# Another instruction order and buffer assignment for a transformer block with local dilated attention and SwiGLU on one core

## The chip, the core and the metric

The kernel runs on one core of a Trainium2 chip. The metric is the device time of one execution in microseconds (us), as the median of several runs. The core has five instruction streams that work side by side, each strictly in its own order: TensorE (PE, matrix products into eight PSUM banks), VectorE (DVE), ScalarE (ACT), GpSimd (POOL) and SyncE (SP), which here does nothing but issue DMA transfers. Streams wait for each other through semaphores.

## What is computed

One block with adaptive layer normalisation, for S = 2048 tokens of D = 512 values in bf16:

```python
mod = silu(c) @ w_mod                 # six vectors: sa, ca, ga, sb, cb, gb
h = layernorm(x) * (1 + ca) + sa
x = x + ga * A(h, wqkv, wo)
h = layernorm(x) * (1 + cb) + sb
x = x + gb * B(h, w1, w3, w2)

def A(x, wqkv, wo):                   # H = 32 heads of 16, W = 8 keys, dilation 2
    q, k, v = split_heads(x @ wqkv)
    # token s sees the tokens s, s-2, ..., s-14; those below 0 are masked
    logits = sum_d(q[s] * k[s - 2*w]) * 16 ** -0.5
    o = sum_w(softmax_w(logits) * v[s - 2*w])
    return merge_heads(o) @ wo

def B(x, w1, w3, w2):                 # F = 1792
    return (silu(x @ w1) * (x @ w3)) @ w2
```

## The kernel before

**Tiling.** The tokens lie in 16 tiles of 128. D has four blocks of 128 and F has 14 units of 128. Everything stays on the chip between the stages, but for v, which goes through a scratch buffer in DRAM so that it can be read back at dilated rows.

**Stages.** First 15 warm-up matmuls run, and `first_modulation` makes two of the six vectors from a load of `w_mod`. Then, for the groups of tiles [0,1], [2,3], [4-7], [8-11], [12-15]: `ln_stats` (statistics on DVE at L579 and L580, the reciprocal root on POOL, normalisation on DVE at L600 or ACT), `ln_T` (transposes on PE, or by DMA for the last group, and modulation), `proj_qk` (matmuls at L722, ACT evacuates them at L730 and L733) and `proj_v` (L749, ACT at L759, a store of each v tile to DRAM at L763).

Attention goes by pairs of tiles, the last block having two pairs. `logits` multiplies q by the eight shifted k on DVE into a buffer pq (L780, 128 x 4096 elements, called pq(T) below) and sums over each head on PE (L791, matmuls on parts of the array, called lg(T)). `shift`, `exps` (ACT, L821) and `softmax` (DVE, L833 to L840) follow. `values` loads the shifted v with four DMAs for each tile (L855), multiplies by the softmax on DVE (L862, called av(T)), sums on PE (L871, called acc), evacuates on ACT (L877), transposes by DMA (L878), applies `wo` (L895, four matmuls of 512 columns) and adds to x on DVE (L899).

The FFN goes by the groups [0,1], [2,3], [4-7], [8-11], [12-15]. `ln_sums` normalises again: L610 (DVE), L614 (ACT, once for each tile of a pair), L620 and L621 (POOL), L622 (DVE), L625 (ACT, once for each tile). `ln_T` transposes: from the third group on by DMA (issued by SP, L127 is the helper's line) with the modulation in four ACT instructions at L648. Each of 14 units (`ffn_unit`) has two halves of four matmuls (L911, `w1` and `w3`); ACT applies silu to the one (L917) and copies the other (L921), and DVE multiplies them (L922); in the last group DVE takes the second one straight from PSUM (L925). `ffn_w2` makes the output of each tile with 14 matmuls (L953; L941 for the last two tiles, in pieces), adds x on DVE (L969) and stores (L971).

The remaining vectors come between: `gate(0)` and the scaling of `wo` (L987) by ga, `modulation(1)` (L494 to L502) with its 1 MB load into `wm_s`, `gate(1)` and the scaling of `w2` (L996) by gb.

**Order.** `_build` (L281) records 1151 operations, each with its engine and the values that it reads and writes. `place` (L147) then deals them out: the list `ORDER` (L1018) names all operations in one sequence, and each engine gets its own in that sequence. The list `SLOTS` (L1064) gives each of 590 short-lived values a buffer out of its pool: 8 PSUM banks, 3 buffers for h, 5 for xn, 6 for v, 4 large ones for pq and shifted v (and 2 more that lie over buffers which are free by then), 20 for FFN products and so on. `synchronize` (L169) works out where an engine must wait for another, from true dependencies and from the buffers' earlier users. An operation's place on its engine and its buffer are thus all that the two lists decide:

```python
self.placed = [self.ops[i] for i in order]
for at, o in enumerate(self.placed):
    o.at = at
    o.pos = len(self.order[o.eng])
    self.order[o.eng].append(o)
    for v in o.vals:
        if v.pool is not None and v.pool.last.get(v.slot) is not v:
            before = v.pool.last.get(v.slot)
            if before is not None:
                o.prev.extend(before.users)
            v.pool.last[v.slot] = v
```

Operations are named by their number in the lists: 44 is the load of `wm_s` for the second modulation, 403 to 406 and 413 to 416 are the loads of shifted v for the tiles 0 and 1, 637 and 627 are the output projections of the tiles 15 and 14 (L895), and 798 is the product (L922) of unit 23, the tenth of the FFN's second group.

Of the kernel before, what the change touches and what calls it, by code (L numbers as in the profile page):

```python
# [280 lines left out]
def _build(p, A_x, A_wqkv, A_wo, B_w1, B_w3, B_w2, c, w_mod, out):  # L281
# [737 lines left out]
    15, 20, 1, 5, 7, 8, 16, 6, 17, 4, 2, 21, 58, 3, 22, 23, 28, 24, 25, 31, 32, 10, 11, 12, 13, 14, 0, 63, 64, 65, 66, 67, 87, 88, 89, 59,  # L1019
    60, 90, 68, 69, 70, 71, 92, 93, 91, 94, 61, 72, 62, 101, 19, 95, 161, 73, 163, 78, 74, 75, 79, 76, 96, 164, 162, 165, 80, 97, 102, 98,  # L1020
    77, 99, 103, 105, 115, 116, 120, 121, 106, 100, 166, 104, 107, 108, 168, 26, 81, 122, 123, 167, 169, 173, 27, 170, 82, 84, 83, 171, 174,
    176, 172, 18, 110, 127, 111, 117, 118, 125, 112, 113, 128, 126, 85, 86, 119, 124, 33, 149, 34, 35, 29, 36, 30, 37, 211, 219, 43, 38,
    212, 209, 150, 151, 217, 155, 156, 152, 157, 175, 158, 159, 153, 109, 114, 9, 180, 181, 154, 41, 49, 210, 192, 129, 195, 186, 187, 160,
    44, 198, 130, 201, 182, 218, 40, 144, 405, 220, 265, 188, 145, 45, 267, 42, 266, 139, 202, 203, 146, 147, 213, 183, 184, 140, 185, 196,
    197, 199, 404, 148, 141, 221, 193, 194, 131, 132, 133, 134, 200, 416, 214, 215, 216, 226, 225, 222, 224, 228, 223, 227, 230, 189, 177,
    233, 232, 231, 178, 234, 276, 413, 229, 274, 277, 268, 235, 415, 236, 325, 377, 142, 205, 206, 135, 179, 275, 414, 332, 334, 136, 137,
    333, 403, 190, 191, 406, 249, 251, 143, 378, 247, 253, 138, 323, 278, 269, 270, 271, 279, 273, 324, 272, 289, 280, 281, 285, 282, 207,
    208, 262, 263, 264, 248, 284, 392, 394, 393, 39, 283, 290, 291, 395, 425, 286, 287, 292, 250, 288, 294, 326, 327, 239, 240, 293, 204,
    396, 335, 397, 398, 54, 252, 243, 241, 242, 423, 237, 238, 254, 245, 295, 314, 399, 384, 259, 336, 400, 337, 338, 340, 339, 328, 401,
    297, 343, 329, 330, 341, 331, 402, 385, 417, 260, 261, 303, 299, 379, 315, 301, 380, 305, 300, 342, 52, 407, 302, 244, 246, 381, 344,  # L1030
    426, 418, 424, 304, 408, 419, 454, 420, 317, 296, 409, 427, 428, 256, 382, 386, 309, 306, 410, 320, 456, 318, 429, 430, 257, 421, 310,
    347, 422, 411, 431, 457, 455, 345, 307, 412, 639, 311, 346, 348, 387, 359, 640, 641, 642, 485, 436, 312, 643, 361, 432, 351, 446, 308,
    360, 363, 644, 646, 383, 437, 444, 298, 362, 652, 645, 255, 365, 651, 321, 653, 433, 647, 353, 447, 487, 258, 352, 354, 648, 650, 445,
    649, 371, 448, 372, 654, 368, 369, 449, 488, 450, 435, 434, 438, 486, 439, 440, 458, 459, 50, 47, 51, 316, 460, 357, 358, 355, 489, 490,
    366, 356, 491, 705, 707, 374, 364, 708, 516, 492, 493, 46, 670, 494, 313, 53, 700, 375, 715, 716, 451, 452, 453, 441, 442, 443, 733,
    349, 671, 48, 461, 462, 717, 388, 706, 350, 734, 660, 477, 735, 463, 709, 701, 718, 719, 55, 736, 737, 465, 468, 672, 467, 370, 464,
    665, 661, 666, 685, 687, 688, 466, 478, 475, 673, 690, 695, 686, 696, 738, 476, 702, 703, 655, 389, 697, 674, 740, 739, 704, 710, 711,
    691, 680, 692, 518, 499, 698, 689, 662, 745, 506, 498, 741, 663, 664, 746, 747, 748, 742, 667, 668, 682, 319, 683, 657, 469, 743, 658,
    744, 495, 712, 497, 713, 714, 720, 722, 721, 675, 723, 724, 677, 678, 676, 496, 479, 656, 659, 509, 681, 774, 754, 776, 679, 684, 759,
    761, 777, 762, 508, 470, 471, 519, 517, 480, 520, 756, 507, 481, 760, 764, 669, 725, 729, 755, 765, 757, 482, 521, 522, 763, 578, 472,  # L1040
    758, 500, 538, 775, 778, 528, 693, 769, 789, 779, 780, 781, 56, 782, 791, 792, 799, 801, 800, 802, 699, 790, 766, 767, 510, 483, 484,
    501, 768, 511, 502, 523, 524, 512, 793, 473, 474, 749, 751, 750, 57, 525, 390, 391, 770, 804, 806, 503, 527, 807, 513, 694, 783, 752,
    809, 810, 794, 795, 796, 827, 828, 829, 830, 831, 529, 547, 784, 771, 772, 773, 530, 797, 504, 505, 730, 805, 808, 785, 514, 832, 834,
    540, 833, 539, 322, 367, 803, 537, 811, 515, 786, 787, 526, 844, 835, 836, 837, 838, 726, 839, 812, 753, 798, 814, 843, 815, 816, 817,
    823, 531, 532, 373, 813, 840, 841, 845, 818, 788, 842, 819, 820, 824, 549, 541, 542, 550, 580, 731, 821, 727, 846, 533, 534, 850, 579,
    548, 581, 586, 596, 595, 849, 825, 551, 552, 559, 560, 535, 569, 582, 561, 536, 732, 584, 376, 848, 847, 851, 901, 902, 861, 863, 570,
    862, 881, 864, 882, 883, 884, 885, 852, 856, 857, 853, 865, 854, 568, 553, 606, 543, 906, 866, 891, 558, 855, 571, 607, 587, 544, 554,
    555, 556, 557, 871, 873, 872, 874, 605, 867, 908, 909, 868, 869, 562, 876, 877, 878, 879, 572, 893, 870, 563, 585, 583, 573, 880, 564,
    822, 588, 907, 910, 545, 911, 546, 903, 894, 630, 892, 565, 937, 574, 575, 912, 939, 858, 589, 590, 615, 895, 859, 875, 896, 938, 940,
    904, 886, 888, 566, 887, 889, 860, 728, 629, 576, 941, 942, 929, 943, 616, 577, 617, 944, 898, 567, 945, 619, 597, 632, 618, 631, 947,  # L1050
    897, 913, 620, 946, 948, 949, 591, 592, 593, 916, 917, 918, 919, 925, 914, 915, 950, 933, 954, 899, 953, 905, 952, 921, 956, 920, 951,
    890, 955, 959, 958, 900, 926, 927, 934, 922, 923, 622, 594, 957, 633, 621, 930, 931, 623, 608, 960, 981, 598, 599, 1016, 1018, 1017,
    1019, 1020, 976, 978, 977, 979, 980, 983, 961, 1021, 986, 987, 962, 984, 988, 996, 997, 971, 1006, 989, 982, 1007, 1008, 1009, 963, 609,
    600, 634, 624, 610, 601, 602, 972, 998, 964, 965, 611, 612, 1001, 1011, 1002, 991, 1026, 999, 1000, 603, 604, 932, 935, 635, 636, 992,
    613, 614, 993, 625, 626, 936, 1047, 924, 973, 1049, 990, 974, 1048, 994, 1050, 1027, 1051, 995, 985, 1010, 1052, 1013, 966, 968, 975,
    969, 1054, 637, 1022, 967, 627, 628, 1023, 1024, 928, 1003, 638, 1012, 1055, 1028, 1064, 1056, 1057, 1058, 1059, 970, 1053, 1039, 1035,
    1043, 1031, 1025, 1063, 1014, 1004, 1060, 1062, 1066, 826, 1061, 1029, 1015, 1065, 1070, 1069, 1030, 1005, 1036, 1044, 1037, 1068, 1032,
# [52 lines left out]
```

## Time and profile before

| | us |
|---|---|
| three runs | 239.56, 241.00, 238.92 |
| their median | 239.56 |
| the profiled execution | 239.86 |
| its span, first to last instruction | 237.7 |

The page of the profile gives, for the profiled execution, the busy time of each engine, the same in 40 slices of the span, the queues of the DMA engines, the chain of work that ended last, and the costliest groups of instructions. In such a group stand the line, engine and operation, the output and its inputs, how many instructions it has, their busy time, the mean of one in ns, and the engine's idle time just before them with what ended most of it. The chain shows where the end of the program comes from:

```profile
PE 68%; DVE 12%; DMA 7%; ACT 7%; issue 3%; POOL 1%; SPq 1%; DVEq 0%
```

Followed back from the last instruction, 68% of the span is work of PE. The other view used below is the timeline, which lists runs of equal instructions with their start, their length from the first start to the last end, engine, line and operation, and in brackets how long the engine had been idle before and what released it.

### The profile page before, as it was taken

How to read it: one execution, taken by the hardware profiler on the slowest of the kernel's cores; microseconds unless marked ns; L12 is line 12 of the kernel's file. 1: busy time of each engine (PE TensorE's matmuls, PEld its weight loads, DVE VectorE, ACT ScalarE, POOL GpSimd, SP SyncE). 2: the span in 40 equal slices, each digit the busy share in tenths (PEclk: the TensorE clock that was granted, in tenths of full speed). 3: DMA queues.
4: the chain of work that ended last, by engine and by line, in shares of the span. 5: the costliest groups of instructions: out<-in, count | busy, mean ns of one | idle time of the engine just before them, and what ended most of it. 6: DMA issues, size and time to landing. Idle time of an engine off the chain costs nothing.

```text
span 237.7 us, 4314 instructions
## 1 busy us (share of the span) xinstructions
PE 229.9 (97%) x1665; PEld 120.7 (51%) x1689; DVE 169.8 (71%) x284; ACT 156.4 (66%) x311; POOL 23.1 (10%) x55
## 2 busy tenths in 40 slices
PE   7899998999999999999999999999999999999996
PEld 2667543544568855754434444444344444444454
DVE  4789998999999999999999847379134424042722
ACT  2289798899989987683689799444757926133100
POOL 8323050001001000030000021000001100000000
PEclk9999999999999999999999999999999999999999
DMA  6999999989999977693897484330032142000002
GB/s 185 341 352 351 238 274 179 188 221 297 327 261 273 285 181 223 139 261 69 205 330 116 124 229 105 103 117 0 3 90 88 44 77 80 0 0 0 3 0 88
DMA packets 44731, 38.31 MB, mean 161 GB/s; under 512 B 19736, under 2 KB 36008, under 8 KB 44712
## 3 DMA queue, kind: packets, MB, share of 16 engines
q1 hardware_dynamic: 44656, 38.04, 63.3%
q8 instruction: 13, 0.21, 0.4%
q14 instruction: 6, 0.05, 0.1%
q10 hardware_dynamic: 56, 0.01, 0.0%
HBM read 29.63 MB, written 4.21 MB: 142 GB/s over the span
## 4 chain that ended last, share of the span: by engine, by line
PE 68%; DVE 12%; DMA 7%; ACT 7%; issue 3%; POOL 1%; SPq 1%; DVEq 0%
PE pall L911 38%; PE pall L953 13%; PE pall L722 5%; DMA sb_wo<-in_A_wo_dram 5%; PE pall L895 4%; DVE sb_vsh L862 3%; PE pall L941 3%; DMA sb_wm_s<-in_w_mod_dram 2%; PE pall L871 2%; PE pall L749 2%; ACT sb_h L648 1%; ACT sb_xn L614 1%; PE pall L791 1%; DVE sb_pq L780 1%; DVE sb_pq L862 1%
## 5 line engine op out<-in xcount | busy, mean ns | idle before, releaser
L911 PE MATMUL pall<-sb_h,sb_w 128*128 128x512 bf16 (+1 forms) x554 | 99.6, 336 | 0.5 <-issue 0.2
L911 PEld LDWEIGHTS pall<-sb_h,sb_w 128*128 128x128 bf16 x560 | 52.2, 98 | 47.1 <-ACT sb_sg L917 5.2
L917 ACT ACTIVATE sb_sg<-pall 128x512 bf16<-128x512 f32 (+1 forms) x70 | 33.9, 516 | 29.6 <-PE pall L911 28.6
L953 PE MATMUL pall<-sb_w,sb_hh 128*128 128x512 bf16 x190 | 43.4, 379 | 0.3
L722 PE MATMUL pall<-sb_h,sb_wqkv 128*128 128x512 bf16 (+1 forms) x157 | 30.4, 336 | 1.3 <-ACT sb_v L759 0.8
L953 PEld LDWEIGHTS pall<-sb_w,sb_hh 128*128 128x128 bf16 x196 | 18.9, 98 | 22.7 <-issue 0.4
L921 ACT ACTIVATE sb_hh<-pall 128x256 bf16<-128x256 f32 (+1 forms) x56 | 26.8, 497 | 3.4 <-PE pall L911 3.0
L922 DVE TENSOR_TENSOR sb_hh<-sb_sg,sb_hh 128x256 bf16<-128x256 bf16 (+1 forms) x56 | 17.7, 351 | 12.8 <-ACT sb_hh L921 12.8
L969 DVE TENSOR_TENSOR sb_o<-pall,sb_x 128x512 bf16<-128x512 f32 (+3 forms) x18 | 10.9, 627 | 18.5 <-PE pall L953 13.7
L722 PEld LDWEIGHTS pall<-sb_h,sb_wqkv 128*128 128x128 bf16 x160 | 14.6, 98 | 14.0 <-ACT sb_v L759 1.3
L925 DVE TENSOR_TENSOR sb_hh<-sb_sg,pall 128x512 bf16<-128x512 bf16 x14 | 9.1, 684 | 16.0 <-PE pall L911 15.9
L648 ACT ACTIVATE sb_h<-sb_h,sb_modc 128x512 bf16<-128x512 bf16 x16 | 11.7, 806 | 11.2 <-DMA sb_h<-sb_xn 11.2
L620 POOL TENSOR_SCALAR sb_rs<-sb_var 128x2 f32<-128x2 f32 x8 | 3.4, 427 | 144.4 <-ACT sb_xn L614 144.4
L862 DVE TENSOR_TENSOR sb_pq<-sb_pq,sb_al 128x4096 bf16<-128x4096 bf16 x7 | 15.8, 2285 | 1.0 <-DMA sb_pq<-v_scratch_dram 1.0
L862 DVE TENSOR_TENSOR sb_vsh<-sb_vsh,sb_al 128x4096 bf16<-128x4096 bf16 x7 | 15.9, 2281 | 0.0
L749 PE MATMUL pall<-sb_wqkv,sb_h 128*128 128x512 bf16 x59 | 15.2, 379 | 0.3 <-issue 0.2
L895 PE MATMUL pall<-sb_wo,sb_ot 128*128 128x512 bf16 x60 | 14.9, 379 | 0.6 <-issue 0.5
L673 ACT ACTIVATE sb_h<-pall,sb_modc 128x256 bf16<-128x256 bf16 (+1 forms) x20 | 12.2, 659 | 2.7 <-DVE sb_modc L522 1.8
L780 DVE TENSOR_TENSOR sb_vsh<-sb_q,sb_kT 128x4096 bf16<-128x4096 bf16 x6 | 13.6, 2286 | 0.4 <-ACT sb_q L730 0.4
L625 ACT ACTIVATE sb_xn<-sb_x,sb_nb,sb_rs 128x512 bf16<-128x512 bf16 x16 | 12.4, 818 | 1.9 <-DVE sb_nb L622 1.7
L614 ACT ACTIVATE sb_xn<-sb_x,sb_nm 128x512 bf16<-128x512 bf16 x16 | 11.4, 716 | 2.7 <-DVE sb_nm L610 2.7
L899 DVE SCALAR_TENSOR_TENSOR sb_x<-pall,sb_x 128x512 bf16<-128x512 f32 x16 | 10.7, 678 | 2.9 <-PE pall L895 2.7
(111 smaller groups left out, 254.5 us busy)
## 6 DMA issues: line engine op xcount, KB each, us to landing
sb_pq<-v_scratch_dram SPq DMA_DIRECT2D x28, 256.0 KB, 6.8
sb_vsh<-v_scratch_dram SPq DMA_DIRECT2D x28, 256.0 KB, 5.0
sb_w<-in_B_w_dram SPq DMA_DIRECT2D x6, 512.0 KB, 6.9
sb_w<-in_B_w_dram SPq DMA_DIRECT2D x6, 384.0 KB, 5.9
v_scratch_dram<-sb_v SPq DMA_DIRECT2D x16, 128.0 KB, 5.8
out_dram<-sb_o SPq DMA_DIRECT2D x14, 128.0 KB, 1.8
sb_wqkv<-in_A_wqkv_dram SPq DMA_DIRECT2D x6, 256.0 KB, 6.2
sb_x<-in_A_x_dram SPq DMA_DIRECT2D x3, 512.0 KB, 7.7
```

The lines of the kernel that those rows point to most:

```text
L614: p.op("act", lambda e, vn=vn, T=T: e.activation(vn.at[:], x_sb[:, T, :], ACT.Square, bias=nm[:, T, :], scale=D ** -0.5, accum_out=var[:, ...
L648: return e.activation(vh.at[:, ft, 0:n * P], vh.at[:, ft, 0:n * P], ACT.Identity, bias=modc[:, 8 * which + ft:8 * which + ft + 1], scale=m ...
L722: ins = e.matmul(bank(vp)[:, 0:n], wqkv[:, t, kind * D + ft * P:kind * D + (ft + 1) * P], vh.at[:, t, 0:n], start=(t == ORDER[0]), stop=(t ...
L749: ins = e.matmul(bank(vp), vh.at[:, t, tt * P:(tt + 1) * P], wqkv[:, t, 2 * D:3 * D], start=(t == ORDER[0]), stop=(t == ORDER[-1]))
L780: return e.tensor_tensor(bass.AP(vp.at, 0, [[8 * D, P], [KT * P, W], [P, KT], [1, P]]), in0, in1, ALU.mult)
L862: return e.tensor_tensor(v_w, v_w, a_w, ALU.mult)
L895: ins = e.matmul(bank(vy), vt.at[:, ft, :], wo[:, ft, :], start=(ft == 0), stop=(ft == KT - 1))
L911: ins = e.matmul(bank(vp)[:, 0:n], wt[:, t, fi * P:(fi + 1) * P], vh.at[:, t, 0:n], start=(t == 0), stop=(t == KT - 1))
L917: p.op("act", lambda e: e.activation(vt.at[:, 0:n], bank(vgp)[:, 0:n], ACT.Silu), c_act(n), k, r=[vgp], w=[vt], table="silu")
L921: p.op("act", lambda e: e.activation(vh_.at[:, 0:n], bank(vup)[:, 0:n], ACT.Copy), c_act(n), k, r=[vup], w=[vh_])
L922: p.op("dve", lambda e: e.tensor_tensor(vh_.at[:, 0:n], vt.at[:, 0:n], vh_.at[:, 0:n], ALU.mult), 60 + n * 69 // 128, k, r=[vt], w=[vh_], ...
L953: ins = e.matmul(bank(vz), vhh[fi].at[:, tt * P:(tt + 1) * P], w2[:, fi, :], start=(fi == 0), stop=(fi == NF - 1))
```

## The change

The code stays as it is. Only the lists `ORDER` and `SLOTS` are replaced: the same 1151 operations in another sequence on all five engines, and other buffers of the same pools for the 590 values. The new sequence was found by a search over cases in which single transfers, drawn at random, come late. The beginnings and ends of the two lists:

```diff
 ORDER = [
-    15, 20, 1, 5, 7, 8, 16, 6, 17, 4, 2, 21, 58, 3, 22, 23, 28, 24, 25, 31, 32, 10, 11, 12, 13, 14, 0, 63, 64, 65, 66, 67, 87, 88, 89, 59,
...
-    1150,
+    10, 6, 11, 20, 3, 5, 1, 2, 0, 4, 21, 58, 22, 23, 87, 88, 89, 90, 28, 24, 25, 31, 32, 59, 63, 64, 65, 66, 67, 68, 69, 60, 92, 93, 94, 95,
...
+    1132, 1127, 1133, 1134, 1128, 1140, 1141, 1142, 1135, 1143, 1129, 1130, 1144, 1145, 1146, 1136, 1137, 1138, 1147, 1148, 1149, 1150,
 ]
 SLOTS = [
-    0, 0, 0, 0, 0, 0, 0, 0, 0, 0, 1, 2, 2, 2, 2, 3, 0, 2, 2, 0, 1, 2, 0, 1, 0, 6, 3, 4, 3, 0, 2, 1, 5, 7, 1, 2, 0, 0, 1, 1, 1, 5, 3, 5, 6,
...
+    0, 0, 0, 0, 0, 0, 0, 0, 0, 0, 1, 1, 3, 3, 3, 3, 0, 1, 7, 0, 1, 1, 0, 2, 5, 0, 4, 3, 2, 0, 4, 2, 7, 1, 1, 7, 0, 1, 0, 6, 1, 2, 7, 4, 3,
...
 ]
```

What that comes to on the engines, as far as the prediction speaks of it:

- On POOL nine of the instructions that make constants and masks stand behind the reciprocal roots of the first two tiles (L584, L586); before, all but one of these nine stood ahead of them.
- On DVE one L579 and two L580 that stood ahead of pq(0) stand behind pq(1).
- On SP the load 44 stood ahead of the eight loads 403 to 406 and 413 to 416, and stands behind them. On PE the second modulation stands, as it did, behind lg(0) to lg(3), acc(0) and acc(1).
- On DVE the product 798 stands directly ahead of av(7), where it stood ahead of av(8). On ACT the copy that it needs stands behind the exponentials of the block of tiles 8 and 9.
- On PE the matmuls of `gate(1)` (L555) stand directly behind lg(1), where matmuls of L663, L722 and L749 stood between; on SP their load `wm_g` stands ahead of seven of the eight v loads as before, and now of all eight.
- On PE one more pair of FFN halves stands ahead of the acc of tile 5, and lg(13) no longer comes right behind lg(10) to lg(12).
- After the last output projection (627 before, 637 now) PE had three FFN halves and the eight blocks of L953 of the fourth group before the fifth group's first L911. Now it has one half and the eight blocks. On DVE one L899 is left at that point instead of two; on ACT one copy L921 stands ahead of the first L625 instead of two, and five evacuations ahead of L614.
- The last outputs' pieces and stores are in another order, and the last piece is the same.

113 rows, old and new, of tables (ORDER, SLOTS) are left out of this document.

## The prediction

> **What bounds the kernel now.** I read the page first: busy shares, then the slices.
>
> ```profile
> span 237.7 us, 4314 instructions
> ...
> PE 229.9 (97%) x1665; PEld 120.7 (51%) x1689; DVE 169.8 (71%) x284; ACT 156.4 (66%) x311; POOL 23.1 (10%) x55
> ...
> PE   7899998999999999999999999999999999999996
> ...
> DVE  4789998999999999999999847379134424042722
> ...
> PEclk9999999999999999999999999999999999999999
> ```
>
> TensorE (PE) is busy in every slice, at the full granted clock. VectorE (DVE) is as full as PE from the fourth slice to the twenty-second, about 20 to 130 us, and half empty after that. A busy PE need not be a PE at its rate, so the view by windows came next. Its columns are the length, then busy time and instructions of PE, weight loads, DVE, ACT and POOL, then clock, DMA share and GB/s.
>
> ```profile
> 20.00:130.00 110.00, 107.67 (x945) 62.05 (x956) 106.69 (x150) 91.78 (x190) 10.26 (x16) 1.00 0.96 231
> 130.00:235.40 105.40, 104.63 (x566) 47.81 (x574) 49.02 (x90) 54.58 (x99) 4.00 (x8) 1.00 0.25 65
> 150.00:160.00 10.00, 9.95 (x47) 4.42 (x46) 4.99 (x6) 3.72 (x6) 0.00 (x0) 1.00 0.45 131
> ```
>
> In the last row PE starts 46 to 47 matmuls of 512 columns in 10.00 us: one costs about 0.216 us and nothing stands between them. The change removes no matmul, so this rate is a floor. PE's idle time is 237.7 - 229.9 = 7.8 us, part of it the start and the tail, and a new order can gain only out of that.
>
> So there are two stretches. Until about 130 us PE, DVE and ACT are all full, and a microsecond that DVE loses reaches PE at the next point where PE has nothing else to do. After that only PE counts, except where it waits for a new group's input. The timeline shows the waits before 130 us:
>
> ```profile
> 23.60 6.73 DVE L780 TENSOR_TENSOR sb_vsh<-sb_q,sb_kT 128x4096 bf16<-128x4096 bf16 x3 [0.45 <-ACT sb_q L730]
> ...
> 37.64 4.49 DVE L862 TENSOR_TENSOR sb_pq<-sb_pq,sb_al 128x4096 bf16<-128x4096 bf16 x2 [1.01 <-DMA sb_pq<-v_scratch_dram]
> ...
> 40.21 1.90 PE L722 MATMUL pall<-sb_h,sb_wqkv 128*128 128x512 bf16 x8 [0.80 <-ACT sb_v L759]
> ...
> 112.94 2.93 ACT L648 ACTIVATE sb_h<-sb_h,sb_modc 128x512 bf16<-128x512 bf16 x4 [3.47 <-DMA sb_h<-sb_xn]
> ...
> 114.50 0.62 PE L791 MATMUL pall<-sb_vshx,sb_E 128*32 128x256 bf16 x16 [0.28 <-DVE sb_vshx L780]
> 115.28 0.81 PE L895 MATMUL pall<-sb_wo,sb_ot 128*128 128x512 bf16 x3 [0.16 <-issue]
> 115.93 2.33 PE L911 MATMUL pall<-sb_h,sb_w 128*128 128x512 bf16 x10
> ```
>
> The last ACT instruction of L648 ends at 112.94 + 2.93 = 115.87, and PE's first matmul of the third FFN group (tiles 4 to 7) starts at 115.93. That handoff has no slack: whatever delays DVE before it delays PE.
>
> The other tight handoff is the last one, to the fifth FFN group (tiles 12 to 15):
>
> ```profile
> 182.27 1.89 PE L895 MATMUL pall<-sb_wo,sb_ot 128*128 128x512 bf16 x7
> ...
> 184.82 0.69 DVE L899 SCALAR_TENSOR_TENSOR sb_x<-pall,sb_x 128x512 bf16<-128x512 f32 x1
> ...
> 185.55 0.17 DVE L610 TENSOR_SCALAR sb_nm<-sb_sx 128x2 f32<-128x2 f32 x1
> ...
> 186.03 0.72 ACT L614 ACTIVATE sb_xn<-sb_x,sb_nm 128x512 bf16<-128x512 bf16 x1
> ...
> 186.59 12.25 PE L953 MATMUL pall<-sb_w,sb_hh 128*128 128x512 bf16 x55
> ...
> 186.74 0.72 ACT L614 ACTIVATE sb_xn<-sb_x,sb_nm 128x512 bf16<-128x512 bf16 x1
> ...
> 187.63 0.22 POOL L620 TENSOR_SCALAR sb_rs<-sb_var 128x2 f32<-128x2 f32 x1 [5.10 <-ACT sb_xn L614]
> 187.93 0.71 POOL L621 TENSOR_TENSOR sb_rs<-sb_rs,sb_cst 128x2 f32<-128x2 f32 x1
> 188.15 1.07 ACT L921 ACTIVATE sb_hh<-pall 128x512 bf16<-128x512 f32 x2
> 188.67 0.16 DVE L622 SCALAR_TENSOR_TENSOR sb_nb<-sb_sx,sb_rs 128x2 f32<-128x2 f32 x1 [2.30 <-POOL sb_rs L621]
> ...
> 189.10 1.52 ACT L625 ACTIVATE sb_xn<-sb_x,sb_nb,sb_rs 128x512 bf16<-128x512 bf16 x2
> ...
> 191.80 1.20 SPq L127 DMA_TRANSPOSE sb_h<-sb_xn  x1
> ...
> 195.82 2.93 ACT L648 ACTIVATE sb_h<-sb_h,sb_modc 128x512 bf16<-128x512 bf16 x4 [4.71 <-DMA sb_h<-sb_xn]
> ...
> 198.81 1.47 PE L911 MATMUL pall<-sb_h,sb_w 128*128 128x512 bf16 x6
> ```
>
> One chain runs from the last output projection (L895, ends 182.27 + 1.89 = 184.16) over DVE, ACT, POOL, DVE, ACT, the SP queue and ACT to 195.82 + 2.93 = 198.75. Meanwhile PE works through the second FFN matmuls of the group before (L953), until 186.59 + 12.25 = 198.84, and it starts the new group at 198.81. Here too the slack is nil.
>
> **The change part by part.** Positions are from the two ORDER lists; nothing is added or removed, so each term is a wait.
>
> *Start.* The first fifteen SP loads and the two of ACT keep their order, as do the opening warm-up matmuls. POOL's masks go behind the first normalisation. The first projections wait for the same modulation load. Cost 0.0 (-0.1 to +0.1).
>
> *First attention tiles.* One layer-norm statistic (L579) and two small aggregations (L580), ahead of pq(0) (L780) before, go behind pq(1). pq(0) can't use that time: it needs all q and k of tiles 0 to 3, and ACT's list up to the last of these holds the same evacuations.
>
> ```profile
> 20.91 1.25 DVE L579 BATCH_NORM_STATS2 sb_st<-sb_x 128x6 f32<-128x512 bf16 x2
> 22.08 0.17 DVE L580 BATCH_NORM_AGGREGATE sb_mv<-sb_st 128x2 f32<-128x6 f32 x1
> ```
>
> ```profile
> sb_wm_s<-in_w_mod_dram SPq DMA_DIRECT2D x1, 1024.0 KB, 8.9
> ```
>
> These three instructions (timeline rows above) are worth 0.62 + 2 x 0.17 = 1.0 us, which DVE idles before 23.6 and does later: +1.0 us, or +1.5 if ACT gets to its last k later. In return the 1024 KB transfer of `wm_s` (row of the DMA issues: 8.9 us to landing) goes from ahead of the eight v loads of tiles 0 and 1 to behind them. At the 231 GB/s of the window row that is some 4.5 us of queue, more than the 1.01 us that DVE waited for these loads at 37.64. That wait should go: -1.0 us. The user of `wm_s` (the second modulation, L501) stays behind the first six tiled groups of L791 and L871 at their new place, and I take it as covered; if the load is late, PE stands for the rest of its 8.9 us, which belongs to the range. PE's gate matmuls (L555), before at 35.17, go directly behind lg(1), whose last matmul was near 29 us; their load was issued at 21.27 and took 9.8 us, to 31.1:
>
> ```profile
> 21.27 0.59 SPq L127 DMA_DIRECT2D sb_wm_g<-in_w_mod_dram  x1
> ...
> 35.17 0.54 PE L555 MATMUL pall<-sb_csz,sb_wm_g 128*128 128x1 bf16 x16
> ```
>
> ```profile
> sb_wm_g<-in_w_mod_dram SPq DMA_DIRECT2D x1, 512.0 KB, 9.8
> ```
>
> On SP it keeps its place, now without the 1024 KB ahead of it, so I land it 4.5 us sooner, at 26.6, in time: 0.0. If nothing is gained there PE waits 31.1 - 29 = 2.1 us; the waits further on that this could use up are 0.80, 0.28 and 0.16 us, which leaves +0.9 us as its end. The sum on DVE's line is 0.0, with -1.0 (pq(0) somewhat earlier) and +1.5 (v loads late anyway) as ends. PE's 0.80 us at 40.21 may go or move, but what PE gains there it gives back at 115.93, since that start hangs on DVE's line.
>
> *Middle, 45 to 115 us.* DVE does the same L780, L862 and softmax work in nearly the same sequence; products of the FFN (L922) move between them. The residual sums (L899) of tiles 6 and 7, from which the 115.93 handoff starts, keep their place on DVE to within one L899 (0.69 us), and the last, tile 7, has the same work ahead of it. lg(13) no longer follows lg(10) to lg(12) directly, so 0.28 + 0.16 us of PE wait at 114.50 and 115.28 can go; PE then waits for L648 instead. Cost 0.0, with the ends carried over from DVE's line.
>
> *Last handoff.* Before, three FFN half-units (4 matmuls each) and the eight L953 blocks follow the last output projection; after, one half-unit and the eight blocks. The chain thus starts 2 x 4 x 0.216 = 1.73 us later against PE, at 184.16 + 1.73 = 185.89. Part of this is absorbed. DVE then has one L899 left, not two: it starts at 185.9, and L610 at 186.66 (0.73 later, as 184.82 to 185.55). L614 follows at 186.85, when L610 is done; before, ACT began 0.48 us after the start of L610. The pair ends at 186.85 + 1.43 = 188.28 against 187.46: +0.82. POOL and L622 follow at once: L622 at 189.49. Before, two copies of L921 (188.15) held L625 until 189.10, 0.27 us after L622's end; after, one copy stands there and is done in time, so L625 starts at 189.67: +0.57. SP's sequence behind it (transpose, store, transpose) is the same, so the last transpose is issued at 192.4. If ACT still has some of the five evacuations that now stand ahead of L614, each about 0.5 us (half of L921's 1.07), the chain is later by up to 0.8 more. Bounds +0.5 and +1.3; I take +0.8, nearer the computed end, since ACT is half idle there. PE's cover ends at 198.8, so the term counts in full.
>
> Against this term speaks a rule of the Trainium skill, "TensorE: Matmul & The Clock Gate", section "Back-to-back issue gap": a stream of 512-column matmuls sustains about 131 ns each, and 216 ns is the gap of isolated ones. By that rule the eight matmuls are 1.05 us, less than what is absorbed, the term is 0.0 and the time 239.6. The window row disagrees with it, at 0.216 in a dense stream.
>
> *End.* The last SP stores and output blocks change their order, but the last PE piece, its L969 and its store are the same: 0.0.
>
> **Sum.** Profiled execution: 239.86 us, span 237.7, so 2.2 us lie around it. 0.0 + 0.0 + 0.0 + 0.8 + 0.0 gives 240.66. That execution is 0.3 us above the median of the three runs, 239.56; against the median: 239.56 + 0.8 = 240.4 us. Its own range, with the ends of DVE's line (-1.0, +1.5; PE's 0.9 is not added, since both would hide behind each other) and of the handoff (+0.5, +1.3), is 239.1 to 242.4.
>
> **Rivals.**
>
> *DVE waits in order for ACT (slower).* The new order puts some L922 products far earlier on DVE, unit 23's directly ahead of av(7) (L862). Each needs ACT's copy, which for unit 23 stands behind the exponentials of tiles 8 and 9 with their two table loads. The chain of waits shows that block:
>
> ```profile
> 86.42 1.28 ACT L821
> 87.71 0.58 ACT pall L821
> ...
> 89.59 0.39 ACT sb_sg L917
> ```
>
> From 86.42 to 89.59 ACT frees no bank: 3.17 us. One more FFN pair, 8 matmuls of 256 columns or about 0.9 us, now stands on PE before the acc group (tile 5) that ACT must evacuate first. So a wait of up to 0.9 us is within the ends above; if ACT is behind by the whole block, DVE loses 3.2 us before 115.93, and PE all of it: 239.56 + 0.8 + 3.2 - 0.4 (PE waits that go) = 243.2 us. It decides from the point where DVE's lag exceeds the 0.44 us that PE can save. For it: three full engines and in-order queues. Against: 0.39 us per evacuation here is less than the 0.43 us of its four matmuls (half of 8 x 0.108), so ACT catches up.
>
> The Trainium skill, "ScalarE: Activation LUTs", section "What ACT_TABLE_LOAD costs", adds a drain of about 1.38 us to each load of 1.28 us. By that rule the block would take 2.8 us more and this rival would end near 246. The chain shows the exponential 0.01 us behind its load, so no drain is paid there.
>
> *The waits vanish (faster).* DVE's 1.01 us and PE's 0.44 us go, pq(0) is not later, and the last chain is absorbed. Then the 115.93 handoff comes 1.0 us sooner: 239.56 - 1.0 = 238.6 us. The spread of the runs before, 238.92 to 241.0, would speak for it if late loads cause it; the last chain speaks against. Over 1% would need 2.4 us out of 7.8 that include start and tail.
>
> *The lists move and nothing else does.* Slack takes it all up: 239.6 us, inside the forecast's range.
>
> **How the numbers follow.** Forecast 0.48, slower rival 0.28, faster rival 0.19, no effect 0.05. The range from 238.3 to 243.4 holds most of each and leaves out about one in ten on each side. One per cent, about what a measurement of this kernel can tell from no change, is 2.4 us: below 237.2 lies only the far end of the faster rival, 0.07; above 242.0 lie the slower rival and the end of the forecast, 0.31; between, 0.62.
>
> **What would show it.** Right: DVE's wait for v loads near 37 us is gone and its idle time before the first L780 grows to about 1.5 us; the third group's first L911 follows L648 at once, within 1 us of 115.9; PE idles 0.5 to 1.3 us at the last handoff, near 199, released by L648. Wrong: no idle time there (the chain was absorbed), DVE idle for ACT's sb_hh between 78 and 95 us (slower rival), or a load late on PE's path, `wm_s` first of all.

## The result and the profile after

The changed kernel takes 242.21 us (median of 16 executions, 241.40 to 245.93), the kernel before beside it 239.87 us (16 executions, 238.78 to 241.72). The ratio is 1.0094, with a 95% interval of 1.0067 to 1.0121: some 2.3 us slower. In four of the 16 executions, all above 244 us, the mean granted clock was 0.993 instead of 1.00; the last section works out what that can be.

The profiled execution took 241.43 us, one of the fastest. Its page, first the span, busy shares and slices:

```profile
span 238.9 us, 4329 instructions
...
PE 231.6 (97%) x1689; PEld 120.2 (50%) x1689; DVE 170.6 (71%) x284; ACT 156.1 (65%) x311; POOL 22.3 (9%) x55
...
PE   7899999997999999999999999999999999999996
...
PEclk9999999999999999999999999999999999999999
```

PE's busy time can't be compared with the 229.9 us of before, whose record lacks 24 matmuls (1665 against 1689). The slices can: a 7 stands in PE's tenth slice, about 54 to 60 us, where the kernel before had a 9. The view by windows gives the size (length; busy time and instructions of PE, weight loads, DVE, ACT, POOL; clock, DMA share, GB/s), for before and then for after:

```profile
40.00:60.00 20.00, 19.53 (x193) 10.13 (x197) 19.63 (x21) 18.70 (x37) 1.23 (x2) 1.00 0.97 225
```

```profile
40.00:60.00 20.00, 18.46 (x189) 9.05 (x188) 19.09 (x21) 16.54 (x32) 1.99 (x2) 1.00 0.79 213
```

PE stands 1.54 us in these 20, against 0.47. The timeline of after shows on what:

```profile
46.23 0.60 ACT L759 ACTIVATE sb_v<-pall 128x512 bf16<-128x512 f32 x1
...
50.05 0.59 SPq L127 DMA_DIRECT2D v_scratch_dram<-sb_v  x1
...
53.36 1.89 PE L722 MATMUL pall<-sb_h,sb_wqkv 128*128 128x512 bf16 x8
...
55.50 1.09 ACT L759 ACTIVATE sb_v<-pall 128x512 bf16<-128x512 f32 x2 [2.01 <-DMA v_scratch_dram<-sb_v]
...
56.64 1.04 PE L722 MATMUL pall<-sb_h,sb_wqkv 128*128 128x512 bf16 x4 [1.39 <-ACT sb_v L759]
```

The ACT instruction at 55.50 evacuates the v of tile 8. It has all its data, but the new SLOTS give it v buffer 0, in which the v of tile 6 has lain since 46.23. SP issues the store of that v only at 50.05, behind four loads of shifted v, and it lands some 5.4 us later. Until then ACT stands for 2.01 us, no PSUM bank comes free, and PE stands for 1.39 us. Buffers 4 and 5 of the six were empty the whole time: their first tenants come at 65.78 and 67.03.

The other places of the prediction, in the same timeline:

```profile
23.38 4.50 DVE L780 TENSOR_TENSOR sb_vsh<-sb_q,sb_kT 128x4096 bf16<-128x4096 bf16 x2 [0.95 <-ACT sb_kT L734]
...
28.49 0.55 PE L555 MATMUL pall<-sb_csz,sb_wm_g 128*128 128x1 bf16 x16
...
34.99 4.49 DVE L862 TENSOR_TENSOR sb_pq<-sb_pq,sb_al 128x4096 bf16<-128x4096 bf16 x2
...
42.56 0.94 PE L497 MATMUL pall<-sb_csz,sb_wm_s 128*128 128x8 bf16 x32
...
53.09 1.28 POOL L620 TENSOR_SCALAR sb_rs<-sb_var 128x2 f32<-128x2 f32 x1 [19.67 <-ACT sb_xn L614]
...
55.20 0.16 DVE L622 SCALAR_TENSOR_TENSOR sb_nb<-sb_sx,sb_rs 128x2 f32<-128x2 f32 x1 [0.91 <-POOL sb_rs L621]
...
113.63 2.93 ACT L648 ACTIVATE sb_h<-sb_h,sb_modc 128x512 bf16<-128x512 bf16 x4 [2.92 <-DMA sb_h<-sb_xn]
...
116.88 2.33 PE L911 MATMUL pall<-sb_h,sb_w 128*128 128x512 bf16 x10
```

VectorE idles 0.95 us before pq(0) and does not wait for the v loads of tiles 0 and 1 (34.99 has no bracket). L555 and L497 don't wait for their loads. VectorE stands 0.91 us for POOL ahead of L622 at 55.20, where it stood 0.30 before; the prediction did not have this. The third FFN group starts at 116.88, 0.95 later than before. It does not follow L648 at once: the last L648 ends at 116.56, 0.32 us earlier, and PE is still busy with older work. The last handoff:

```profile
185.14 1.89 PE L895 MATMUL pall<-sb_wo,sb_ot 128*128 128x512 bf16 x8
...
187.73 12.25 PE L953 MATMUL pall<-sb_w,sb_hh 128*128 128x512 bf16 x56
...
188.14 0.17 DVE L610 TENSOR_SCALAR sb_nm<-sb_sx 128x2 f32<-128x2 f32 x1
...
191.25 1.52 ACT L625 ACTIVATE sb_xn<-sb_x,sb_nb,sb_rs 128x512 bf16<-128x512 bf16 x2 [0.85 <-DVE sb_nb L622]
...
193.96 1.97 SPq L127 DMA_TRANSPOSE sb_h<-sb_xn  x1
...
197.07 2.93 ACT L648 ACTIVATE sb_h<-sb_h,sb_modc 128x512 bf16<-128x512 bf16 x4 [4.29 <-DMA sb_h<-sb_xn]
...
200.05 1.25 PE L911 MATMUL pall<-sb_h,sb_w 128*128 128x512 bf16 x5
```

L648 ends at 200.00 and PE starts at 200.05, 0.07 after the last L953 ends at 199.98. The chain is still without slack, but PE loses about 0.1 us more there than before, and not 0.8. The 56 matmuls of L953 take (12.25 - 0.16) / 56 = 0.216 us each, as before.

### The profile page after: what moved, and what is told of

The parts are those of the page before. It is cut to its first block, busy times and chain, and to the rows that moved or that the text cites. A ratio compares the mean times of both kernels' runs of the same rounds, so it can differ in the third digit from the quotient of the medians.

```text
span 238.9 us, 4329 instructions
## 1 busy us (share of the span) xinstructions
PE 231.6 (97%) x1689; PEld 120.2 (50%) x1689; DVE 170.6 (71%) x284; ACT 156.1 (65%) x311; POOL 22.3 (9%) x55
## 5 line engine op out<-in xcount | busy, mean ns | idle before, releaser
L911 PE MATMUL pall<-sb_h,sb_w 128*128 128x512 bf16 (+1 forms) x560 | 101.1, 337 | 0.1
L911 PEld LDWEIGHTS pall<-sb_h,sb_w 128*128 128x128 bf16 x560 | 52.3, 98 | 47.7 <-ACT sb_sg L917 5.6
L917 ACT ACTIVATE sb_sg<-pall 128x512 bf16<-128x512 f32 (+1 forms) x70 | 34.6, 520 | 24.9 <-PE pall L911 24.3
L953 PE MATMUL pall<-sb_w,sb_hh 128*128 128x512 bf16 x196 | 44.1, 379 | 0.0
L722 PE MATMUL pall<-sb_h,sb_wqkv 128*128 128x512 bf16 (+1 forms) x160 | 31.3, 337 | 1.6 <-ACT sb_v L759 1.4
L921 ACT ACTIVATE sb_hh<-pall 128x256 bf16<-128x256 f32 (+1 forms) x56 | 26.1, 507 | 9.1 <-PE pall L911 9.1
L953 PEld LDWEIGHTS pall<-sb_w,sb_hh 128*128 128x128 bf16 x196 | 18.8, 98 | 22.7 <-DVE sb_hh L922 0.6
L722 PEld LDWEIGHTS pall<-sb_h,sb_wqkv 128*128 128x128 bf16 x160 | 14.6, 98 | 13.4 <-ACT sb_v L759 2.5
L780 DVE TENSOR_TENSOR sb_vsh<-sb_q,sb_kT 128x4096 bf16<-128x4096 bf16 x9 | 20.4, 2280 | 0.9 <-ACT sb_kT L734 0.9
L648 ACT ACTIVATE sb_h<-sb_h,sb_modc 128x512 bf16<-128x512 bf16 x16 | 11.9, 804 | 10.5 <-DMA sb_h<-sb_xn 10.5
L620 POOL TENSOR_SCALAR sb_rs<-sb_var 128x2 f32<-128x2 f32 x8 | 3.8, 480 | 147.4 <-ACT sb_xn L614 147.4
L895 PE MATMUL pall<-sb_wo,sb_ot 128*128 128x512 bf16 x64 | 16.0, 380 | 0.7 <-DMA sb_ot<-sb_oa 0.7
L862 DVE TENSOR_TENSOR sb_pq<-sb_pq,sb_al 128x4096 bf16<-128x4096 bf16 x7 | 15.9, 2280 | 0.0
L749 PE MATMUL pall<-sb_wqkv,sb_h 128*128 128x512 bf16 x64 | 15.8, 379 | 0.0
L625 ACT ACTIVATE sb_xn<-sb_x,sb_nb,sb_rs 128x512 bf16<-128x512 bf16 x16 | 12.4, 817 | 3.7 <-DVE sb_nb L622 3.7
L899 DVE SCALAR_TENSOR_TENSOR sb_x<-pall,sb_x 128x512 bf16<-128x512 f32 x16 | 10.8, 679 | 3.9 <-PE pall L895 3.9
L614 ACT ACTIVATE sb_xn<-sb_x,sb_nm 128x512 bf16<-128x512 bf16 x16 | 11.4, 716 | 0.9 <-DVE sb_nm L610 0.9
L579 DVE BATCH_NORM_STATS2 sb_st<-sb_x 128x6 f32<-128x512 bf16 x16 | 10.5, 677 | 1.8 <-DMA sb_x<-in_A_x_dram 1.8
```

Of the source, the lines that this page charges most:

```text
L625: p.op("act", lambda e, vn=vn, T=T: e.activation(vn.at[:], x_sb[:, T, :], ACT.Identity, bias=nb[:, T, :], scale=rs[:, NT + T, :]), c_act(5 ...
L648: return e.activation(vh.at[:, ft, 0:n * P], vh.at[:, ft, 0:n * P], ACT.Identity, bias=modc[:, 8 * which + ft:8 * which + ft + 1], scale=m ...
L722: ins = e.matmul(bank(vp)[:, 0:n], wqkv[:, t, kind * D + ft * P:kind * D + (ft + 1) * P], vh.at[:, t, 0:n], start=(t == ORDER[0]), stop=(t ...
L749: ins = e.matmul(bank(vp), vh.at[:, t, tt * P:(tt + 1) * P], wqkv[:, t, 2 * D:3 * D], start=(t == ORDER[0]), stop=(t == ORDER[-1]))
L780: return e.tensor_tensor(bass.AP(vp.at, 0, [[8 * D, P], [KT * P, W], [P, KT], [1, P]]), in0, in1, ALU.mult)
L862: return e.tensor_tensor(v_w, v_w, a_w, ALU.mult)
```

## The experiments

All kernels have the same operations; only places in the order and buffer numbers differ. Each ratio is to the kernel before, executed on the same chip.

**Another buffer for tile 8's v.**

```diff
-SLOTS[95] = 0
+SLOTS[95] = 4
```

> The new order with one buffer number changed: tile 8's v goes into v buffer 4, free at that time, instead of buffer 0, whose tenant (tile 6) is still being stored to DRAM. Theory (the wait for that store costs most of the loss): PE's 1.39 us before L722 near 56.6 and the 0.3 to 0.5 us behind it go, and the time falls by 1.5 to 2.3 us, to 0.998 to 1.003 of the kernel before. Rival (VectorE's line sets the third FFN group's start anyway): the wait goes, the start near 116.9 stays within 0.3 us, and the time stays above 1.007 of the kernel before.

Measured: 241.45 us, ratio 1.0053 (1.0027 to 1.0079). The timeline of this kernel, at the evacuation and at what it still waits for:

```profile
52.99 1.07 ACT L759 ACTIVATE sb_v<-pall 128x512 bf16<-128x512 f32 x2
...
82.08 2.29 DVE L862 TENSOR_TENSOR sb_pq<-sb_pq,sb_al 128x4096 bf16<-128x4096 bf16 x1 [0.43 <-DMA sb_pq<-v_scratch_dram]
...
104.51 2.29 DVE L862 TENSOR_TENSOR sb_pq<-sb_pq,sb_al 128x4096 bf16<-128x4096 bf16 x1 [0.59 <-DMA sb_pq<-v_scratch_dram]
...
172.66 0.81 PE L911 MATMUL pall<-sb_h,sb_w 128*128 128x512 bf16 x3 [0.41 <-ACT sb_oa L877]
```

The wait is gone, and so are all executions above 243 us. The third FFN group starts at 116.33, 0.55 earlier than with the change, where the rival had at most 0.3. But the time falls by less than the theory said: in this trace VectorE waits for later v loads, at 82.08 and 104.51, and PE waits at 172.66. Neither theory is right as it stands.

**The store earlier, with the buffers of the change.** Only SP's order differs:

```diff
-258, 445, 437, 444, 446, 261, 447, 435, 316
+258, 445, 261, 437, 444, 446, 447, 435, 316
```

> The new order and its own buffers, with one SP step moved: the store of tile 6's v, issued at 50.05 us behind three v loads of tiles 2 and 3, is issued three loads (about 1.9 us) earlier. Theory (ACT's v evacuation of tile 8 waits for the landing of that store): the store lands 1.9 us sooner, ACT's 2.01 us and PE's 1.39 us near 56 almost go, no execution has the longer wait, and the time comes to 1.003 to 1.007 of the kernel before, as with the other buffer (1.0053). Rival (the transfers are limited by the DMA engines' total work, so the place in the queue hardly matters): the wait stays at 1 us or more and the time at 1.008 or more.

Measured: 240.55 us (239.62 to 241.62), ratio 1.0026 (0.9998 to 1.0054). Timeline:

```profile
48.11 0.62 SPq L127 DMA_DIRECT2D v_scratch_dram<-sb_v  x1
...
53.39 1.07 ACT L759 ACTIVATE sb_v<-pall 128x512 bf16<-128x512 f32 x2
...
116.10 5.35 PE L911 MATMUL pall<-sb_h,sb_w 128*128 128x512 bf16 x23 [0.49 <-ACT sb_h L648]
...
172.60 0.81 PE L911 MATMUL pall<-sb_h,sb_w 128*128 128x512 bf16 x3 [0.57 <-ACT sb_oa L877]
```

One store, issued 1.9 us sooner, takes away 0.68% of the 0.94%, and this interval does not overlap with that of the change. Against the other buffer, which takes away 0.41% by removing the same wait, the difference is within the intervals. PE now waits for L648 at 116.10, as the prediction said it would at this handoff.

**The store later.** The same step, three places the other way:

```diff
-446, 261, 447, 435, 316, 434
+446, 447, 435, 316, 261, 434
```

> The new order with the store of tile 6's v issued three SP steps (about 1.9 us) later than there, instead of earlier. Theory (each microsecond by which that store lands later is one of PE's wait, and a PE wait of near 3 us is followed by some microseconds at a lower granted clock, as the run with the restored last handoff shows): PE waits 3 to 3.5 us near 58 us, the granted clock in the next 5 us is about 0.7, and the time is 1.020 to 1.027 of the kernel before in nearly all executions. Rival (what that run lost came from its changed last handoff): 1.9 us more than the new order at most, 1.013 to 1.018, at a granted clock of 1.00 throughout.

Measured: 246.77 us, ratio 1.0261 (1.0214 to 1.0307). Timeline, then windows:

```profile
58.34 1.08 ACT L759 ACTIVATE sb_v<-pall 128x512 bf16<-128x512 f32 x2 [4.50 <-DMA v_scratch_dram<-sb_v]
...
59.48 1.89 PE L722 MATMUL pall<-sb_h,sb_wqkv 128*128 128x512 bf16 x4 [3.87 <-ACT sb_v L759]
```

```profile
56.00:59.00 3.00, 0.00 (x0) 0.00 (x0) 3.00 (x2) 0.66 (x2) 0.00 (x0) 0.90 1.07 335
59.00:60.00 1.00, 0.52 (x2) 0.25 (x3) 1.00 (x1) 1.00 (x3) 0.00 (x0) 0.50 1.11 336
...
64.00:65.00 1.00, 1.00 (x3) 0.29 (x2) 0.00 (x0) 0.86 (x2) 0.00 (x0) 0.50 0.13 43
65.00:66.00 1.00, 1.00 (x6) 0.47 (x5) 0.00 (x0) 0.47 (x1) 0.00 (x0) 0.89 0.01 2
```

PE waits 2.48 us more than with the change (3.87 against 1.39), and the clock granted is 0.50 from shortly before the wait's end to about 5.7 us after it. The time goes the way of the store in both directions, so that the wait for it is a main part of the loss is shown. How large a part is not: it is 0.41% by the other buffer and 0.68% by the earlier store.

**The last handoff restored, on the change itself.** On PE, 627 and 637 stand two FFN half-units earlier; on DVE, 628, 638 and 1055 move with them:

```diff
-PE: 966, 968, 1013, 627, 637, 1028
+PE: 966, 627, 637, 968, 1013, 1028
-DVE: 985, 970, 980, 628, 638, 1055
+DVE: 985, 628, 638, 1055, 970, 980
```

> The new order with only its last handoff restored: the two last output projections stand two FFN half-units earlier on PE again, so that three half-units and the eight L953 blocks follow them. Theory of the prediction (1.73 us less cover costs 0.8 us): 0.8 us faster than the new order, about 1.006 of the kernel before. Rival (the chain was shortened by as much as the cover, as the trace shows a gap of only 0.24 against 0.13 us): within 0.3 us of the new order, 1.008 to 1.011 of the kernel before.

Measured: 246.39 us, ratio 1.0240 (1.0203 to 1.0277), which neither theory can give. The trace says that it isn't the handoff: timeline and windows near 58 us, where this kernel's order is that of the change,

```profile
58.54 1.04 PE L722 MATMUL pall<-sb_h,sb_wqkv 128*128 128x512 bf16 x4 [2.80 <-ACT sb_v L759]
```

```profile
58.50:60.00 1.50, 1.31 (x7) 0.58 (x8) 1.50 (x1) 1.50 (x3) 0.00 (x0) 0.90 1.10 305
60.00:61.00 1.00, 1.00 (x5) 0.36 (x3) 1.00 (x2) 0.86 (x2) 0.00 (x0) 0.50 1.09 331
...
63.00:64.00 1.00, 1.00 (x6) 0.41 (x5) 0.45 (x1) 0.65 (x2) 0.00 (x0) 0.94 1.10 366
```

The same store was issued 0.7 us later here, at 50.75, and ACT's wait for it ended 6.65 us after that, 1.2 us more than with the change. PE waited 2.80 us, and the clock went to 0.50 for about 3.4 us. So this run could not settle the handoff, and it was made again without that wait.

**The last handoff restored, with the earlier store.** The two edits above together.

> The kernel with the earlier store of tile 6's v, and the last handoff restored: two more FFN half-units behind the last output projections, as in the kernel before. Theory of the prediction (1.73 us less cover costs 0.8 us): 0.8 us below the kernel with the earlier store alone, 0.999 to 1.000 of the kernel before. Rival (the chain got shorter by as much; the swap makes PE wait for ACT's copies at 187 to 192 us instead): no gain, or up to 0.9 us slower, 1.002 to 1.006.

Measured: 242.38 us, ratio 1.0088 (1.0051 to 1.0124), against 1.0026 without the restored handoff. Timeline of PE:

```profile
183.26 1.90 PE L895 MATMUL pall<-sb_wo,sb_ot 128*128 128x512 bf16 x7 [0.16 <-ACT sb_hh L921]
...
187.58 1.04 PE L911 MATMUL pall<-sb_h,sb_w 128*128 128x512 bf16 x4 [0.69 <-ACT sb_hh L921]
188.56 12.26 PE L953 MATMUL pall<-sb_w,sb_hh 128*128 128x512 bf16 x55
200.69 3.63 PE L911 MATMUL pall<-sb_h,sb_w 128*128 128x512 bf16 x16
```

With the old cover the new group starts without any wait, but there was little to win, and PE now waits for ACT's copies to free banks, at 183.26 and 187.58, ahead of the projections and behind them. From the wait at 172.6 to the new group's start it takes 200.69 - 172.62 = 28.07 us, against 199.47 - 172.60 = 26.87 with the earlier store alone. The prediction's 0.8 us is refuted.

**The wait at 172 us.** ACT's fourth evacuation of an attention sum waits there for a transposing DMA, since there are two buffers `oa`; a bank stays taken, and PE stands. In the change ACT's wait is:

```profile
172.21 0.60 ACT L877 ACTIVATE sb_oa<-pall 128x512 bf16<-128x512 f32 x1 [0.51 <-DMA sb_ot<-sb_oa]
```

PE's 20 matmuls there, which at 0.216 us each are 4.32 us, take 173.84 - 169.17 = 4.67 us in the change and 173.35 - 168.40 = 4.95 with the earlier store: the wait is there in both, and larger in the second. The edit, on top of the earlier store:

```diff
-ACT: 982, 635, 1004, 992
+ACT: 982, 1004, 992, 635
-PE: 1011, 1026, 603, 1021
+PE: 1011, 1021, 1026, 603
```

> The kernel with the earlier store of tile 6's v, and near 172 us two swaps: on ACT the evacuations of units 50 and 48 of the fourth group's FFN go ahead of the attention evacuation of tile 15 (L877), which waits there for the transposing DMA that holds its buffer; on PE a matmul group whose bank is free goes ahead of the one whose bank that evacuation frees. Theory (PE's 0.57 us at 172.6, which the kernel before lacks, is what is left of the loss): the wait goes and the time falls by 0.4 to 0.7 us, to 0.9995 to 1.001 of the kernel before. Rival (the last handoff's chain takes it up): the gap at 199.5 grows by as much, and the time stays at 1.002 to 1.003.

Measured: 240.48 us (239.83 to 241.48), ratio 1.0011 (0.9987 to 1.0036). In the timeline PE runs through, and ACT has other work while the DMA lands:

```profile
168.32 5.36 PE L911 MATMUL pall<-sb_h,sb_w 128*128 128x512 bf16 x23
173.51 1.03 PE L895 MATMUL pall<-sb_wo,sb_ot 128*128 128x512 bf16 x4
```

The wait is gone. What this alone is worth, 0.15% between the two ratios, is less than their intervals. With both edits the new order can't be told from the kernel before, and with the earlier store alone its interval already just reaches 1.

**Single parts on the kernel before.** First the evacuation of tile 9, whose wait of 0.80 us PE has at 40.21, gets a free buffer (two others are exchanged for it):

```diff
-SLOTS[97], SLOTS[117], SLOTS[119] = 1, 1, 5
+SLOTS[97], SLOTS[117], SLOTS[119] = 5, 5, 1
```

> The kernel before with three buffer numbers changed: the v of tiles 9 and 12 in buffer 5, of tile 13 in buffer 1, so that tile 9's evacuation near 39.6 us waits for no store. Theory of the prediction (what PE gains at 40.2 it gives back at the third group's start, which hangs on VectorE): the 0.8 us wait goes and the time stays within 0.3 us of the kernel before. Rival (every such wait counts in full): 0.8 us faster, 0.9967.

Measured: 240.65 us, ratio 0.9991 (0.9962 to 1.0020). PE's wait is gone, and there is no gain; but the interval also holds the rival's 0.9967. In the trace VectorE waits at tile 3's v loads, and PE behind it:

```profile
36.45 4.49 DVE L862 TENSOR_TENSOR sb_pq<-sb_pq,sb_al 128x4096 bf16<-128x4096 bf16 x2
...
57.95 4.49 DVE L862 TENSOR_TENSOR sb_vsh<-sb_vsh,sb_al 128x4096 bf16<-128x4096 bf16 x2 [1.50 <-DMA sb_vsh<-v_scratch_dram]
```

```profile
60.30 0.61 PE L871 MATMUL pall<-sb_vsh,sb_ind 128*32 128x512 bf16 x8 [0.88 <-DVE sb_vsh L862]
```

The third group's first L911 comes 116.50 - 23.43 = 93.07 us after the first L780, against 92.33 before. This does not show that the freed wait moved, though. VectorE reaches tile 3's loads 1.1 us sooner because the wait of 1.01 us at 37.64 does not occur here (36.45 has no bracket), and nothing ahead of 38 us differs from the kernel before. So the wait at 37.64 is there in one execution of this order and not in another.

Second, the 1 MB load alone behind the eight v loads (SP: 44 behind 406).

> The kernel before with only the 1 MB load for the second modulation moved on SP from ahead of the eight v loads of tiles 0 and 1 to behind them. Theory of the prediction: VectorE's 1.01 us wait for the v loads near 37.6 us goes and the third FFN group starts up to 1.0 us sooner, 0.996 of the kernel before. Rival (the wait moves, or the late load makes PE's second modulation wait): within 0.3 us of the kernel before, or slower, with a PE wait at L494 or L497.

Measured: 241.39 us, ratio 1.0042 (1.0013 to 1.0070). The eight v loads land sooner, in 6.0 us at the median against 9.3 before, and there is no wait near 37 us; but as the run above shows, that can be so without this edit. A larger wait stands further on:

```profile
59.51 4.49 DVE L862 TENSOR_TENSOR sb_vsh<-sb_vsh,sb_al 128x4096 bf16<-128x4096 bf16 x2 [2.16 <-DMA sb_vsh<-v_scratch_dram]
```

The time is the rival's: by itself this part of the change makes the old order slower. PE has no wait at L494 or L497. Why tile 3's loads land that late there was not followed up.

Third, on top of the first, tile 3's v loads go ahead:

```diff
-SP: 436, 446, 437, 444, 255, 447, 258, 445, 435, 434
+SP: 446, 444, 447, 255, 445, 436, 437, 435, 258, 434
```

> The kernel before with tile 9's v in a free buffer (the three buffer numbers of the earlier run) and, on SP, the four v loads of tile 3 ahead of those of tile 2 and of the store of tile 5's v, so that the last of tile 3's is issued some 1.8 us sooner. Theory (up to 116 us VectorE's line sets the time; freeing PE's wait alone moved the loss to VectorE's 1.50 us wait for the v loads of tile 3 at 57.95): that wait falls to 0.3 us or less, the third FFN group starts about 1 us sooner, and the time is 0.994 to 0.997 of the kernel before, faster than both kernels. Rival (the loads are limited by the work of the DMA engines, whatever their order): VectorE waits as long, for the loads of tile 2 or for others, and the time stays within 0.3 us, 0.998 to 1.002.

Measured: 240.02 us beside 240.57, ratio 0.9978 (0.9949 to 1.0007). VectorE's 1.50 us wait is gone from the timeline. From the first L780 to the third group's first L911 it takes 116.33 - 24.74 = 91.59 us, less than before (92.33); but the first L780 itself stands 1.14 us later than before, ahead of all that differs. The time lies between the two theories and its interval holds 1: a version that clearly beats both kernels was not found.

**VectorE's other waits in the new order.** On top of the other buffer for tile 8's v, the statistics go back ahead of pq(0) (DVE: 332, 333, 324 ahead of 392), and then also L840 (433) behind pq(6) (485).

> The first cure (tile 8's v in buffer 4) and, on VectorE, one L579 and two L580 back ahead of the first L780, where they were. Theory of the prediction (these were worth 1.0 us that VectorE now idles and does later): VectorE's line is 0.3 to 1.0 us earlier at 107 us and the time 0.3 to 1.0 us below that of the first cure, 1.001 to 1.004 of the kernel before. Rival (VectorE meets its next wait, for POOL at 54 us or for v loads, and loses it there): within 0.3 us of the first cure, 1.004 to 1.007.

> The kernel of the run before and, on VectorE, tile pair 2's transpose L840 (0.71 us) moved from ahead of pq(6) to behind it, as before the change, where VectorE idled 0.90 us for POOL's L620 and L621. Theory (each wait on VectorE's line up to 116 us counts): the idle time before L622 falls from 0.90 to about 0.2 us and the time by a further 0.5 to 0.7 us. Rival (POOL's two instructions wait for VectorE's long L780 to end, and are only pushed later): L621 ends as late after L840 as it did, the idle time stays over 0.6 us, and the time stays within 0.3 us.

Measured: 241.38 us, ratio 1.0047 (1.0018 to 1.0076), and 240.95 us, 1.0051 (1.0026 to 1.0075), beside 1.0053 without either. The first kernel's VectorE timeline, and the second's:

```profile
28.06 0.69 DVE L803 TENSOR_REDUCE sb_mx<-pall 128x64 f32<-128x512 f32 x1 [0.65 <-PE pall L791]
```

```profile
52.10 2.29 DVE L780 TENSOR_TENSOR sb_vsh<-sb_q,sb_kT 128x4096 bf16<-128x4096 bf16 x1 [0.29 <-PE pall L791]
55.30 0.16 DVE L622 SCALAR_TENSOR_TENSOR sb_nb<-sb_sx,sb_rs 128x2 f32<-128x2 f32 x1 [0.28 <-POOL sb_rs L621]
```

The waits aimed at do shrink (0.90 to 0.28 us for POOL), and others appear: for lg(1) at 28.06, for lg of tiles 4 and 5 at 52.10. No gain shows in the times; the 0.3 us that the first theory allowed at least can't be excluded at these intervals.

## Why the prediction was right, and where its steps were not

The time lies in the upper part of the range and on the side of the forecast, but the sum was not the one that it gave: the one term that was not nothing, +0.8, was nearly absent, and a wait priced at nothing took its place. That the number came out right is in good part luck.

*Start: 0.0.* It holds as far as the traces go: in the first 40 us PE has one wait of 0.60 us for the first modulation's load, in place of one of 0.56 for VectorE, and a new one of 0.20.

*First attention tiles: +1.0 and -1.0.* Neither term is shown. VectorE idles 0.95 us before pq(0) against 0.45, where about 1.5 was forecast; but this idle time scatters: it is 0.51 and 1.48 in two other traces with the old order up to there (the experiment with tile 9's buffer and the one on top of it), and 0.32 to 1.20 in six with the new one. The 1.01 us for the v loads of tiles 0 and 1 are gone with the change, and the loads land sooner, 5.1 to 7.7 us after issue against 7.7 to 12.8. But those same two traces of the old order lack this wait as well: a wait seen in one execution was priced as if it stood in all. L497 and L555 found their loads landed. From the first L780 to the third group's first L911 passed 115.93 - 23.60 = 92.33 us before and 116.88 - 23.38 = 93.50 with the change. Without the new wait it is 116.10 - 23.38 = 92.72 (earlier store) and 116.33 - 22.98 = 93.35 (other buffer): 0.4 to 1.0 us longer than before, within the ends given around 0.0.

*Middle: 0.0.* This is the step that failed. The text said that PE's 0.80 us at 40.21 "may go or move" and be given back. It was itself ACT's wait for a v buffer, as the timeline of before shows:

```profile
39.56 0.60 ACT L759 ACTIVATE sb_v<-pall 128x512 bf16<-128x512 f32 x1 [0.84 <-DMA v_scratch_dram<-sb_v]
```

What takes its place in the new order wasn't looked up: which v takes over whose buffer, and where on SP the store stands that frees it. There a wait of the same kind stands at 56.64. It is 1.39 us in the profiled execution and 2.80 us in that of the restored handoff, and cost between 0.41% (1.0094 - 1.0053) and 0.68% (1.0094 - 1.0026), some 1.0 to 1.6 us. In the profiled executions 0.95 us of the 1.2 us by which the span grew are there at the third group's start. That PE's gains up to here are given back was not shown by the experiment with tile 9's buffer, though its time shows none; that losses are not given back is shown. Of the 0.44 us that PE was to save, the 0.16 at 115.28 were no wait: that row has three of the four matmuls, and one is missing in the record.

*Last handoff: +0.8.* Measured about 0.1; that PE would show no idle time there is one of the prediction's own signs of being wrong. The start was 1.73 us later against PE, as worked out: from the end of L895 to the end of L953 it was 198.84 - 184.16 = 14.68 us, and is 199.98 - 187.03 = 12.95. The chain's steps up to the last transpose were mis-sized little: that is issued 193.96 - 187.03 = 6.93 us after the projection, forecast 192.4 - 185.89 = 6.5. The size that was wrong is the DMA's, taken over as constant: from the last transpose's issue to L648 passed 195.82 - 191.80 = 4.02 us before, 197.07 - 193.96 = 3.11 now. It is no scatter: this leg is 3.0 to 3.3 us in all nine traces of the new order and its variants, and 3.9 to 4.4 in the four of the old. Why it is shorter stays open. And the order as it was before is no cure, since it brings waits for ACT's copies.

*End: 0.0.* From the fifth group's start to the end of the span it was 237.7 - 198.81 = 38.89 us, and is 238.9 - 200.05 = 38.85.

*The rivals.* Of VectorE waiting in order for ACT's copies nothing is seen between 78 and 95 us; the time was near that rival's, the mechanism was another. That the waits vanish was half so: they vanish, and the next ones take their place. The rule of 131 ns for a matmul, set against the last handoff's term, is contradicted as before (0.216 us).

*What stays open.* After the earlier store 0.26% is left, some 0.6 us, and its interval just includes no difference. The wait at 172.6 is part of it by the trace, but its worth was not resolved from zero.

## What to carry to other kernels

A buffer that is stored by DMA is free when the store has landed, so a new order has to be read together with the buffers: for each reuse, who holds the buffer, where on its queue the releasing transfer stands, and how late it may land; one store three places earlier took away most of what this change lost. When a wait is said to move, the place where it goes to has to be priced too, and a chain's DMA legs belong into the sum as a range, not as the one value that a trace shows. A wait on a load that one trace shows should be looked for in a second execution before it is priced: here it was absent from two of three. A stretch in which PE already stands for more than a microsecond on one transfer is worth slack, since the price of a longer wait can jump.

## What the hardware showed that was not expected

The price of a PE wait is not its length. Behind the change's wait of 1.39 us the granted clock stays 1.00; with one of 2.80 us it was 0.50 for about 3.4 us, and with one of 3.87 us for about 6.8 us. The windows above give the ends: 58.50:60.00 at 0.90 holds 0.3 us at 0.50 and 63.00:64.00 at 0.94 holds 0.12, so 59.7 to 63.1; in the same way 58.4 to 65.2 for the longer wait. At 0.50 a 512-column matmul takes twice its 0.216 us: four take 1.89 us at 59.48, and 1.04 at 56.64 in the change. With the wait of 2.80 us the drop comes 1.2 us after PE has resumed at 58.54, with that of 3.87 us it comes 1.1 us before PE resumes. The Trainium skill, "TensorE: Matmul & The Clock Gate", section "What's actually happening", describes a gate that halves the clock by activity in windows of about 3.4 us that don't start with the kernel. The lengths of the slow stretches, 3.4 and 6.8 us, agree with one and two such windows; that 2.80 us of waiting are enough is shorter than the gap of about 3.4 us that the page's section "HAM oscillation — how this bites in real kernels" gives, and the trace decides.

One stretch of 3.4 us at 0.50 lowers the mean clock of an execution of 243 us by 3.4 x 0.5 / 243 = 0.7%, to 0.993. That is the mean of the profiled execution with the 2.80 us wait, and of the four long executions of the change; the one with two stretches has 0.986. The four were not profiled, so that they had such a wait is argued, not shown. One execution of the old order with only the load moved has 0.993 too (243.61 us), so other waits may do the same.

POOL's L620, 128x2 elements, took 0.22 us near the end of both kernels and 1.28 us at 53.09 in the changed one, where it starts under VectorE's L780 of 52.05 and ends at 54.37, 0.07 us after that does. The same holds in other traces: 1.71 us at 105.17 with the other buffer, ending 0.08 us after VectorE's L862 of 104.51. It looks as though POOL is held until VectorE's product ends; what holds it was not tried.
